# The value tensor of four attention heads: loaded as float32 from another queue and cast on ScalarE, with two buffers instead of three

## The chip, the cores and the metric

The kernel runs on one core of a Trainium2 chip. The core has five engines that run their own instruction streams: TensorE (PE, matrix products), VectorE (DVE), ScalarE (ACT), GpSimd (POOL) and SyncE (SP). Data comes from HBM into the on-chip memory (SBUF) through 16 DMA engines, which all queues share. Transfers can be issued from POOL, whose queue is called software_dynamic in the profile and can change the type of the data on the way, or from SP, whose queue is called hardware_dynamic and copies without a change of type. The metric is the device time of one execution in microseconds (us).

## The reference

The kernel computes an attention block followed by a "soft" mixture of experts. All inputs and the output are float32.

```python
q, k, v: (8 batches, 8 heads, 576 positions, 64)
scores = q @ k.T / 8
# heads 0..3 ("plain"):   position i sees i-31 .. i
# heads 4..7 ("dilated"): position i sees i, i-4, i-8, .. within 128
x = softmax(masked scores) @ v          # -> (4608, 512), heads side by side
logits = x @ phi                        # (4608, 32 slots), 8 experts x 4 slots
slot_input = softmax(logits, over the 4608 rows).T @ x
slot_out[e] = relu(slot_input[e] @ w1[e]) @ w2[e]   # w1 512x1024, w2 1024x512
out = softmax(logits, over the 32 slots) @ slot_out # (4608, 512)
```

## The kernel before

**Units.** The attention is cut into 32 units, four for each batch: two heads each, in the order plain, dilated, plain, dilated (`unit`, L201). The main loop (L475) is a software pipeline. In the turn of unit u it computes the scores of u+1, the weighted values of u (`values`, L324), the exponentials and masks of u+1 (`softmax_parts`, L276), and the transposes of q and k of u+2 (`transposes`, L207); the mixture's logits, row sums and slot sums (`front_logits`, `front_rows`, `front_slots`) follow one batch later. After the loop come the experts (`expert_in`, `expert_out`) and the 40 output tiles (L582 to L600), which SP stores.

**Loads.** Nearly all data is loaded by POOL, float32 in HBM and float16 in SBUF. `load_batch(b)` (L146) issues q and k of the plain heads, then v of the plain heads in five transfers (L168), then q and k of the dilated heads (L163 again), then v of the dilated heads: `vd` (L177) for positions that fill the first 128 rows of four, and `v2r` (L177) for the rest. `load_w(e)` (L192) issues w1 and w2 of one expert, 1 MB each as float16 (L196 and L197). The tiles are eight buffers called home; three of them carry batches in turn and are reused for weights later, so a load into a home waits until the transposes of the batch that was there are done. v of the plain heads goes to one of three `vp` tiles, each with a column of ones that is set once (L121). `v2r` has one buffer: its next load waits until VectorE has copied the last one out.

**Order.** The table `after` (L453) says after which unit each load is issued: batches 0, 1, 2 and expert 0 before the loop; batch 3 after unit 2; batch 4 and expert 1 after unit 6; batch 5 after 10; batch 6 and expert 2 after 14; batch 7 and experts 3 and 4 after 18; experts 5, 6, 7 after 22, 26, 30. The framework that builds the program then orders the instructions of each engine by its own estimate of when they can start, so that an instruction which must wait can be passed by a later one of the same engine. Once built, each engine takes its list strictly in order. In the kernel before, POOL's list is the order of the program text. Each POOL transfer has one of eight semaphores in turn, so that the ninth waits for the first to land.

**Spreading v of the dilated heads.** `spread_v(b)` (L184) copies `vd` and `v2r` on VectorE into the layout that the products need (L187). It stands in the turn of unit 4(b-1)+1, one batch ahead of its use. VectorE takes its list in order, so everything behind such a copy waits for the transfer that the copy waits for.

Of the kernel before, what the change touches and what calls it, by code (L numbers as in the profile page):

```python
# [9 lines left out]
FP32 = mybir.dt.float32  # L10
# [5 lines left out]
B = 8  # L16
H = 8
S = 576
D = 64
# [11 lines left out]
NKB = 5  # L31
# [2 lines left out]
RD, ND = 8, 72  # L34
CL = S // DIL
NU = 4 * B
NV = 3


def constants():  # L40
# [10 lines left out]
def kernel(  # L51
# [10 lines left out]
    nc = tc.nc  # L62
# [17 lines left out]
        out=phi4, in_=phi_sb[:, :, None, :].broadcast_to([128, 4, 4, N_SLOTS])  # L80
# [5 lines left out]
    def kept(shape, name, dt=FP16):  # L86
        return keep.tile(shape, dt, name=name, tag=name)
# [14 lines left out]
    kTd = kept([128, S + 80], "kTd")  # L102
    vp = [kept([128, NKB, 4, D + 1], f"vp{i}") for i in range(NV)]
    vd = [kept([128, 16, D + 1], f"vd{i}") for i in range(2)]
# [10 lines left out]
    for i in range(2):  # L115
# [3 lines left out]
        nc.vector.memset(Er[i][64:128, 8, :], 0.0)  # L119
    for i in range(NV):  # L120
        nc.vector.memset(vp[i][:, :, :, D : D + 1], 1.0)  # L121
# [6 lines left out]
    small = ctx.enter_context(tc.tile_pool(name="small", bufs=2))  # L128
    x_pool = ctx.enter_context(tc.tile_pool(name="x", bufs=2))
    xT_pool = ctx.enter_context(tc.tile_pool(name="xT", bufs=1))  # L130
    vraw_pool = ctx.enter_context(tc.tile_pool(name="vraw", bufs=1))

    big = tc.alloc_tile_pool(name="big", bufs=1)
# [12 lines left out]
    def load_batch(b):  # L146
        t = homes[b_home[b]]
        parts = {}
        at = 0
        for nm, ten, hs, rows, parts_n in (  # L150
            ("qp", q, 0, RP, NP), ("kp", k, 0, RP, NP), ("qd", q, 4, RD, ND), ("kd", k, 4, RD, ND),
        ):
            n = 4 * rows * D
            parts[nm] = t[0:parts_n, at : at + n].rearrange("p (h x) -> p h x", h=4)
            at += n
            src = ten[b, hs : hs + 4].rearrange("h (p r) d -> p h (r d)", r=rows)
            if b == 0 and hs == 0:
                for i in range(2):
                    nc.gpsimd.dma_start(
                        out=parts[nm][:, 2 * i : 2 * i + 2], in_=src[:, 2 * i : 2 * i + 2]  # L160
                    )
            else:
                nc.gpsimd.dma_start(out=parts[nm], in_=src)  # L163
            if nm == "kp":
                vt = vp[b % NV]
                for kb in range(NKB):
                    n_k = 128 if kb < 4 else 64
                    nc.gpsimd.dma_start(  # L168
                        out=vt[0:n_k, kb, :, 0:D],
                        in_=v[b, 0:4, 128 * kb : 128 * kb + n_k, :].rearrange("h p d -> p h d"),  # L170
                    )
        for nm, r0, n_p, dst in (("vd", 0, 128, vd), ("v2", 384, 48, v2)):
            if nm == "vd":
                vr = t[:, 7168:8192].rearrange("p (h x) -> p h x", h=4)
            else:
                vr = vraw_pool.tile([128, 4, 4 * D], FP16, name=f"v2r{b}", tag="v2r")
            nc.gpsimd.dma_start(  # L177
                out=vr[0:n_p],
                in_=v[b, 4:8, r0 : r0 + 4 * n_p, :].rearrange("h (p r) d -> p h (r d)", r=4),
            )  # L180
            parts[nm] = (vr, n_p, dst[b % 2])
        raws[b] = parts

    def spread_v(b):  # L184
        for nm in ("vd", "v2"):
            vr, n_p, dst = raws[b][nm]
            nc.vector.tensor_copy(  # L187
                out=dst[0:n_p, :, 0:D],
                in_=vr[0:n_p].rearrange("p h (r d) -> p (h r) d", r=4),
            )  # L190
# [10 lines left out]
    def unit(u):  # L201
        b, i = divmod(u, 4)
        return b, (0, 2, 1, 3)[i]
# [3 lines left out]
    def transposes(u):  # L207
        b, hp = unit(u)
        for nm in ("q", "k"):
            if nm == "q":  # L210
                dst = qT_pool.tile([128, S], FP16, name=f"qT{u}", tag="qT")
                qTs[u] = dst
            else:
                dst = kTp if hp < 2 else kTd
                kTs[u] = dst
            if hp < 2:
                raw = raws[b][nm + "p"]
                rg = ring.tile([128, RP, NP], FP16, name=f"rg{nm}{u}", tag="ring")
                for r in range(RP):
                    for h in range(2):  # L220
                        nc.tensor.transpose(  # L221
                            rg[64 * h : 64 * h + 64, r, :],
                            raw[:, 2 * hp + h, D * r : D * r + D],
                            ident[0:NP, 0:NP],
                        )
                nc.scalar.copy(  # L226
                    out=dst[:, 0:S].rearrange("c (p r) -> c p r", r=RP),
                    in_=rg.rearrange("c r p -> c p r"),
                )
            else:  # L230
                raw = raws[b][nm + "d"]
                rg = ring.tile([128, 2, 4, ND], FP16, name=f"rg{nm}{u}", tag="ring")
                for h in range(2):
                    for a in range(2):
                        for cc in range(2):
                            nc.tensor.transpose(  # L236
                                rg[:, a, 2 * h + cc, :],
                                raw[:, 2 * (hp - 2) + h, 128 * (2 * a + cc) : 128 * (2 * a + cc) + 128],
                                ident[0:ND, 0:ND],
                            )  # L240
                nc.vector.tensor_copy(  # L241
                    out=dst[:, 0:S].rearrange("c (g p a) -> c g p a", g=4, a=2),
                    in_=rg.rearrange("c a g p -> c g p a"),
                )

    def scores(u):
        b, hp = unit(u)
        qT, kT = qTs[u], kTs[u]
        tiles = []
        for part in range(2):  # L250
            st = ps_s.tile([128, 2, 512], FP32, name=f"s{u}_{part}", tag="s")
            if hp < 2:
                todo = [(160 * i, 128 * i, 128 * i, QW) for i in range(3)] if part == 0 else [
                    (0, 384, 384, QW), (QW, 512, 512, 64)]
            else:
                todo = []
                for cc in range(2):
                    c0 = CL * (2 * part + cc)
                    todo.append((CL * cc, c0, c0, 128))
                    todo.append((CL * cc + 128, c0 + 96, c0 + 128, 16))  # L260
            for at, k0, q0, n in todo:
                for g in range(2):
                    nc.tensor.matmul(  # L263
                        st[:, g, at : at + n],
                        kT[64 * g : 64 * g + 64, k0 : k0 + 128],
                        qT[64 * g : 64 * g + 64, q0 : q0 + n],
                        start=True,
                        stop=True,
                    )
            tiles.append(st)  # L270
        return tiles
# [52 lines left out]
    def values(u):  # L324
# [7 lines left out]
        for half in range(2):  # L332
# [4 lines left out]
            for i, blk in enumerate(blocks):  # L337
                for h in range(2):
                    if plain:
                        P, vt = Pp, vp[b % NV]  # L340
                        mms.append((i, h, P[:, h, blk, 0:128], vt[:, blk, hl + h, :]))
# [123 lines left out]
    def issue(u):  # L465
        for kind, i in after.get(u, ()):
            (load_batch if kind == "b" else load_w)(i)

    issue(-1)
    transposes(0)  # L470
    spread_v(0)
    transposes(1)
    st = scores(0)
    softmax_parts(0, st)
    for u in range(NU + 5):  # L475
        if u + 1 < NU:
            st = scores(u + 1)
        if u < NU:
            values(u)
        if u + 1 < NU:  # L480
            softmax_parts(u + 1, st)
        if u + 2 < NU:
            transposes(u + 2)
        b, ph = divmod(u - 4, 4)
        if 0 <= b < B:
            if ph == 1:
                front_logits(b)
            elif ph == 2:
                front_rows(b)
            elif ph == 3:  # L490
                front_slots(b)
        if 0 <= u - 1 < NU:
            x_transposes(u - 1)
        if u % 4 == 1 and u // 4 + 1 < B:
            spread_v(u // 4 + 1)
        issue(u)
        if u < 4:
            nc.vector.memset(hTp[u], 0.0)

# [82 lines left out]
    for b in range(B):  # L582
        for t in range(NKB):
# [6 lines left out]
            if n % 2 == 0:  # L590
                nc.scalar.activation(  # L591
                    out=ot[0:ns], in_=fp[0:ns], func=AF.Copy, scale=rrow[0:ns, col : col + 1]
                )
            else:
                nc.vector.tensor_scalar(  # L595
                    out=ot[0:ns], in0=fp[0:ns], scalar1=rrow[0:ns, col : col + 1],
# [35 lines left out]
```

## Time and profile before

| | |
|---|---|
| time, median of 3 runs | 215.36 us (214.96 to 216.22) |
| the profiled execution: its time, its span | 216.12 us, 214.3 us |
| mean granted TensorE clock | 0.804 |
| PE busy | 145.2 us (68%) |
| DVE busy | 138.2 us (64%) |
| ACT busy | 92.5 us (43%) |
| POOL busy (issuing transfers) | 77.3 us (36%) |
| read from HBM, written to it | 63.07 MB, 9.44 MB |
| software queue (POOL) | 50336 packets, 31.47 MB |
| hardware queue (SP) | 6208 packets, 9.60 MB |

The span runs from the first to the last instruction; the device time has 1.8 us more around it. The bytes of a queue are those written, so a float32 load that ends as float16 counts half of what it reads. A row of the profile names a source line, the engine, the operation, the tile written and the tiles read, then the busy time and the mean duration of one, then the idle time of that engine just before, with what ended it. The share of a DMA queue is the sum of its packets' durations over 16 engines; it can exceed 100% because an engine has more than one packet under way.

### The profile page before, as it was taken

To read this page: it belongs to the slowest core of one execution; us is meant where nothing else is said; L and a number is where in the kernel's file an instruction comes from. 1 tells how busy PE (TensorE), PEld (TensorE's weight loads), DVE (VectorE), ACT (ScalarE), POOL (GpSimd) and SP (SyncE) were. 2 spreads that over 40 slices of the span, in tenths; PEclk is the share of its full clock that TensorE was granted. 3 is DMA by queue.
4 is the path that set the end of the run, shared out by engine and by line. 5 is a ranking of instruction groups with operands and counts; after the bars stand their busy time and mean duration, and the time that the engine had idled before them with its cause. 6 is when DMAs were issued, how large, how long until landed. Compare 5 with 4: busy or idle time off the path is not lost.

```text
span 214.3 us, 5426 instructions
## 1 busy us (share of the span) xinstructions
PE 145.2 (68%) x2192; PEld 100.0 (47%) x2192; DVE 138.2 (64%) x429; ACT 92.5 (43%) x169; POOL 77.3 (36%) x110
## 2 busy tenths in 40 slices
PE   5448778287609669768767708687886698678740
PEld 4336667165507556556655606566763433211100
DVE  2745987579337997978798419889775301645551
ACT  2234357064604574571744801574542022445550
POOL 7679847512668612747711660300300000000000
PEclk9999999889655997995898755997579669955555
DMA  6999999999999999999999999999999990599995
GB/s 88 163 172 127 179 177 162 205 206 153 151 174 145 200 208 190 146 174 150 202 207 195 136 195 207 213 207 212 206 212 208 213 175 6 197 323 351 356 322 216
DMA packets 56569, 41.41 MB, mean 193 GB/s; under 512 B 23264, under 2 KB 47840, under 8 KB 56544
## 3 DMA queue, kind: packets, MB, share of 16 engines
q0 software_dynamic: 50336, 31.47, 109.3%
q1 hardware_dynamic: 6208, 9.60, 13.0%
q8 instruction: 17, 0.28, 0.5%
q14 instruction: 8, 0.07, 0.1%
HBM read 63.07 MB, written 9.44 MB: 338 GB/s over the span
## 4 chain that ended last, share of the span: by engine, by line
DMA 44%; PE 15%; DVE 13%; issue 12%; POOL 8%; ACT 3%; SPq 2%; DVEq 0%; ACTq 0%; POOLq 0%
DMA home<-in_k_dram 21%; DMA vp<-in_v_dram 7%; DMA out_dram<-ot 6%; DMA home<-in_v_dram 5%; DMA home<-in_q_dram 4%; PE l L392 3%; PE h L531 3%; POOL home L163 3%; DVE ot L595 2%; SPq L599 2%; DVE x L355 2%; PE rgx L374 2%; DVE qT L241 2%; PE sop L555 2%; PE s L263 1%
## 5 line engine op out<-in xcount | busy, mean ns | idle before, releaser
L282 ACT ACTIVATE pr<-s 128x960 f16<-128x960 f32 (+1 forms) x64 | 41.6, 703 | 38.7 <-issue 30.9
L168 POOL DMA_DIRECT2D vp<-in_v_dram x40 | 29.2, 738 | 23.9 <-DMA home<-in_moe_w_dram 11.5
L355 DVE TENSOR_TENSOR x<-o,rc 128x384 f16<-128x384 f32 x64 | 29.6, 485 | 0.3
L350 PE MATMUL o<-vp,Pp 128*128 128x65 f16 x288 | 16.6, 219 | 18.8 <-DVE Pp L288 17.8
L350 PEld LDWEIGHTS <-Pp 128*128 128x128 f16 x288 | 13.5, 113 | 22.6 <-DVE Pp L288 20.7
L374 PE MATMUL rgx<-ident,x 128*128 128x128 f16 x160 | 17.2, 250 | 8.8 <-ACT qT L226 6.5
L595 DVE TENSOR_SCALAR ot<-f,rrow 128x512 f32<-128x512 f32 (+1 forms) x20 | 14.7, 748 | 12.4 <-DMA out_dram<-ot 10.1
L588 PE MATMUL f<-so,ET 128*128 128x512 f16 (+1 forms) x40 | 18.2, 512 | 6.2 <-DVE ot L595 2.8
L399 ACT ACTIVATE ET<-l 128x288 f16<-128x288 f32 x16 | 6.6, 410 | 33.7 <-PE l L392 33.6
L591 ACT ACTIVATE ot<-f,rrow 128x512 f32<-128x512 f32 (+1 forms) x20 | 13.5, 685 | 15.5 <-DMA out_dram<-ot 11.3
L374 PEld LDWEIGHTS <-x 128*128 128x128 f16 x160 | 13.3, 113 | 11.7 <-issue 9.7
L236 PEld LDWEIGHTS <-home 72*128 72x128 f16 x256 | 12.5, 111 | 12.6 <-issue 9.0
L187 DVE COPY vd<-home 128x1024 f16<-128x1024 f16 x8 | 3.4, 425 | 19.6 <-DMA home<-in_v_dram 19.6
L163 POOL DMA_DIRECT2D home<-in_q_dram x15 | 10.8, 721 | 14.3 <-DMA home<-in_moe_w_dram 13.7
L392 PE MATMUL l<-xT,phi 128*128 128x288 f16 x64 | 14.4, 378 | 1.9 <-DVE qT L241 1.6
L350 PEld LDWEIGHTS <-P 128*128 128x128 f16 x256 | 12.3, 106 | 7.1 <-DVE P L305 5.1
L305 DVE TENSOR_TENSOR P<-pr,mask 128x512 f16<-128x512 f16 x32 | 13.4, 420 | 3.0 <-ACT pr L282 3.0
L221 PEld LDWEIGHTS <-home 96*64 96x64 f16 x384 | 13.1, 140 | 4.3 <-issue 1.8
L236 PE MATMUL rgk<-ident,home 72*128 72x72 f16 x128 | 8.5, 221 | 9.3 <-DVE xT L384 8.4
L350 PE MATMUL o<-vd,P 128*128 128x65 f16 x128 | 11.4, 209 | 3.6 <-DVE P L305 3.6
L588 PEld LDWEIGHTS <-ET 128*128 128x128 f16 (+1 forms) x40 | 4.1, 107 | 20.1 <-issue 19.5
L196 POOL DMA_DIRECT2D home<-in_moe_w_dram x8 | 6.1, 757 | 20.1 <-DVE P L305 12.2
(79 smaller groups left out, 286.4 us busy)
## 6 DMA issues: line engine op xcount, KB each, us to landing
home<-in_moe_w_dram POOLq DMA_DIRECT2D x16, 1024.0 KB, 17.8
out_dram<-ot SPq DMA_DIRECT2D x32, 256.0 KB, 3.3
home<-in_q_dram POOLq DMA_DIRECT2D x15, 288.0 KB, 7.8
home<-in_k_dram POOLq DMA_DIRECT2D x15, 288.0 KB, 8.1
home<-in_v_dram POOLq DMA_DIRECT2D x8, 256.0 KB, 7.9
vp<-in_v_dram POOLq DMA_DIRECT2D x32, 64.0 KB, 9.1
out_dram<-ot SPq DMA_DIRECT2D x8, 128.0 KB, 3.3
v2r<-in_v_dram POOLq DMA_DIRECT2D x8, 96.0 KB, 7.5
```

Of the source, the lines that this page charges most:

```text
L163: nc.gpsimd.dma_start(out=parts[nm], in_=src)
L168: nc.gpsimd.dma_start(out=vt[0:n_k, kb, :, 0:D], in_=v[b, 0:4, 128 * kb : 128 * kb + n_k, :].rearrange("h p d -> p h d"),)
L236: nc.tensor.transpose(rg[:, a, 2 * h + cc, :], raw[:, 2 * (hp - 2) + h, 128 * (2 * a + cc) : 128 * (2 * a + cc) + 128], ident[0:ND, 0:ND],)
L282: nc.scalar.activation(out=pr[:, :, 0:n], in_=st[:, :, 0:n], func=AF.Exp, scale=SCALE)
L305: nc.vector.tensor_tensor(out=P1[:, part].rearrange("p c e t -> p e c t"), in0=src[:, :, :, 0:128], in1=bc(mask[:, None, None, 0:128], [12 ...
L350: nc.tensor.matmul(ot[:, i, h, :], lhs, rhs, start=(n == 0), stop=(n == len(mms) - 1))
L355: nc.vector.tensor_tensor(out=x[:, blocks[0] : blocks[0] + nb, D * hl : D * hl + 2 * D].rearrange("p t (h d) -> p t h d", h=2), in0=ot[:, ...
L374: nc.tensor.transpose(rg[:, 128 * blk : 128 * blk + 128], x[:, blk, hl : hl + 128], ident)
L392: nc.tensor.matmul(lp, phi4[:, kc].rearrange("p a s -> p (a s)"), xT[:, kc, 288 * c : 288 * c + 288], start=(kc == 0), stop=(kc == 3),)
L588: nc.tensor.matmul(fp[0:ns], ET[:, r0 : r0 + ns], so, start=True, stop=True)
L591: nc.scalar.activation(out=ot[0:ns], in_=fp[0:ns], func=AF.Copy, scale=rrow[0:ns, col : col + 1])
L595: nc.vector.tensor_scalar(out=ot[0:ns], in0=fp[0:ns], scalar1=rrow[0:ns, col : col + 1], scalar2=None, op0=ALU.mult,)
```

## The change

v of the plain heads no longer goes through POOL's queue. `load_vp(b)` issues the five transfers on SP, as float32, into a staging tile `v32`, of which there is one. `cast_vp(b)` copies it on ScalarE into the `vp` tile, in two instructions (128 rows of 1024 values, 64 rows of 256 values). There are two `vp` tiles instead of three, and two memsets fewer on VectorE (L121 and L122 of the third tile). v of batches 0 and 1 is loaded before the loop, that of batch b+2 after the cast of batch b+1, in the turn of unit 4b+2. The list `after` is unchanged.

```diff
-NV = 3
+NV = 2
@@ pools
+    v32_pool = ctx.enter_context(tc.tile_pool(name="v32", bufs=1))
@@ load_batch
-            if nm == "kp":
-                vt = vp[b % NV]
-                for kb in range(NKB):
-                    n_k = 128 if kb < 4 else 64
-                    nc.gpsimd.dma_start(
-                        out=vt[0:n_k, kb, :, 0:D],
-                        in_=v[b, 0:4, 128 * kb : 128 * kb + n_k, :].rearrange("h p d -> p h d"),
-                    )
@@ after load_batch
+    v32s = {}
+
+    def load_vp(b):
+        t = v32_pool.tile([128, NKB, 4, D], FP32, name=f"v32_{b}", tag="v32")
+        v32s[b] = t
+        for kb in range(NKB):
+            n_k = 128 if kb < 4 else 64
+            nc.sync.dma_start(
+                out=t[0:n_k, kb],
+                in_=v[b, 0:4, 128 * kb : 128 * kb + n_k, :].rearrange("h p d -> p h d"),
+            )
+
+    def cast_vp(b):
+        t = v32s.pop(b)
+        vt = vp[b % NV]
+        nc.scalar.copy(out=vt[:, 0:4, :, 0:D], in_=t[:, 0:4])
+        nc.scalar.copy(out=vt[0:64, 4, :, 0:D], in_=t[0:64, 4])
@@ before the loop
     issue(-1)
+    load_vp(0)
     transposes(0)
+    cast_vp(0)
+    load_vp(1)
     spread_v(0)
@@ in the loop
         issue(u)
+        if u % 4 == 2 and u // 4 + 1 < B:
+            cast_vp(u // 4 + 1)
+            if u // 4 + 2 < B:
+                load_vp(u // 4 + 2)
```

## The prediction

> **What bounds the kernel now.** I read the slices of the page first, then the DMA queues, VectorE's waits, and the timelines of VectorE and POOL towards the end of the attention.
>
> ```profile
> DMA  6999999999999999999999999999999990599995
> GB/s 88 163 172 127 179 177 162 205 206 153 151 174 145 200 208 190 146 174 150 202 207 195 136 195 207 213 207 212 206 212 208 213 175 6 197 323 351 356 322 216
> ...
> q0 software_dynamic: 50336, 31.47, 109.3%
> ...
> DMA 44%; PE 15%; DVE 13%; issue 12%; POOL 8%; ACT 3%; SPq 2%; DVEq 0%; ACTq 0%; POOLq 0%
> ```
>
> From 5 to 177 us the DMA engines never rest. They run at about 210 GB/s written where only weights move and at 130 to 180 where batches move. No compute engine is near full; transfers make up 44% of the chain that ended last. So until 177 us the order in which data comes off the software queue sets the pace. VectorE's waits show where the arithmetic feels it:
>
> ```profile
> DVE vd L187 <- DMA home<-in_v_dram: 19.6, 6, 6.1
> ```
>
> VectorE, in order, stands 19.6 us at the copy of `vd`, 6.1 us the longest time. Its timeline has the last one, batch 7, and the copy of `v2r`, the last piece of that batch:
>
> ```profile
> 121.64 0.18 DVE L354 RECIPROCAL rc<-o 128x6 f32<-128x6 f32 x1
> 127.97 0.43 DVE L187 COPY vd<-home 128x1024 f16<-128x1024 f16 x1 [6.15 <-DMA home<-in_v_dram]
> ...
> 134.86 0.47 DVE L187 COPY v<-v2r 48x1024 f16<-48x1024 f16 x1
> ```
>
> Up to 127.97 the arithmetic waits for batch 7; the second copy at 134.86 finds its data there. From then on only arithmetic is on the path: attention to 166, experts to 183, output tiles to 214.3. From 134.86 to the end is 79.4 us. POOL's timeline tells what had been sent by then:
>
> ```profile
> 119.56 0.77 POOL L177 DMA_DIRECT2D home<-in_v_dram  x1 [0.63 <-DMA home<-in_k_dram]
> 120.62 0.60 POOL L177 DMA_DIRECT2D v2r<-in_v_dram  x1 [0.29 <-DVE P L313]
> 121.40 0.75 POOL L196 DMA_DIRECT2D home<-in_moe_w_dram  x1 [0.18 <-issue]
> 122.52 0.89 POOL L197 DMA_DIRECT2D home<-in_moe_w_dram  x1 [0.38 <-DMA vp<-in_v_dram]
> ```
>
> All eight batches and three experts (0, 1, 2); the weights of expert 3 come behind batch 7.
>
> **The change, part by part.**
>
> *POOL issues 40 transfers less.* The row of L168 has 29.2 us for them. They are taken off no path: POOL waits for landings, not the other way round (13.7 and 11.5 us of its idle time end with a weight's landing). Worth nothing by itself, and covered by the engines' 9s; if these had gaps, it would be worth up to 0.74 us a transfer.
>
> *POOL's list is reordered; this decides.* In the built program the list is no longer the order of the text. With three `vp` waits a batch gone, the builder moves weights ahead of pieces of batches that must wait. The list towards its end, in transfers:
>
> ```
> home(b5) q k q k, vd(b5), vd(b6), w1 w2 of expert 2, v2r(b5),
> q k q k (b6), vd(b7), w1 w2 of expert 3, w1 of expert 4, v2r(b6),
> q k q k (b7), w2 of expert 4, w1 of expert 5, v2r(b7),
> w2 of expert 5, experts 6 and 7
> ```
>
> The software queue delivers in the order of issue: before, the weights issued between two batches held the next batch up, as the 6.10 us and 6.15 us stops at `vd` show. So `v2r` of batch 7 now lands behind all of batches 0 to 7 and five and a half experts, where it was three. VectorE's list still has its copy at the same place, ahead of the masks of unit 26 (before: 134.86). Price: a weight pair is 2.10 MB written (two of 1024 KB). The windows of the trace, with the last two columns the DMA share and GB/s written, give the rate:
>
> ```profile
> 140.00:170.00 30.00, 22.61 (x363) 17.21 (x364) 21.56 (x72) 13.26 (x29) 1.64 (x2) 0.79 1.18 209
> 29.20:31.20 2.00, 1.55 (x27) 1.38 (x24) 1.51 (x6) 0.97 (x2) 0.72 (x1) 1.00 2.07 156
> ```
>
> 2.10 MB / 209 GB/s = 10.0 us an expert. A batch follows by difference: 127.97 - 2 (start) - 3 x 10.0 = 96.0 us for eight, 12.0 us a batch with its plain v.
>
> *Plain v goes to the hardware queue, as float32.* Per batch 2304 rows of 256 B, read as before, but written as 256 B instead of 128 B. Old price: in the window 29.2 to 31.2, nearly all v, 1731 packets under 512 B pass in 2 us, so 2304 take at most 2.7 us; with the few larger ones in it, 2.5 us. The new price is in no row. Low end: 0.59 MB read at the weights' rate (209 GB/s written is 418 read) is 1.4 us. High end: the old packets' own duration, 207% x 16 x 2 us / 1854 = 36 ns, without their twofold overlap: 2304 x 36 ns / 16 = 5.2 us. Nearest are the constants, the hardware queue's only loads:
>
> ```profile
> q1 hardware_dynamic: 822, 0.12, 0.6%
> ```
>
> 0.6% of 16 x 126 us over 822 packets of the stretch 2 to 128 us is 15 ns; 2304 x 15 ns / 16 = 2.2 us. I take 2.2, so 0.3 us less a batch.
>
> *The rest of a batch.* It costs 12.0 - 2.5 = 9.5 us now. By bytes, 2.95 MB read at 418 GB/s, it would be 7.1. Part of the difference comes from POOL's eight places being filled with five small transfers; with six a batch instead of eleven some comes back. Between 9.5 (nothing) and 7.1 (all) I take 9.3, near the present row, as q and k of 72 partitions stay as they are. A batch is then 9.3 + 2.2 = 11.5 us.
>
> *The sum.* `v2r` of batch 7 lands at 2 + 8 x 11.5 + 5.5 x 10.0 = 149 us; the copy was at 134.86: 14.1 us late. Before it, `v2r` of batch 6, behind seven batches, `vd` of batch 7 (1.6 us) and four and a half experts, lands at 2 + 80.5 + 1.6 + 45 = 129 us. One batch of arithmetic takes 16.0 us where nothing waits (the masks of unit 12 to those of unit 16, 73.26 to 89.29), so this stop alone would set 145 to 146.5 with the casts, less than 149. From the copy to the end it is 79.4 us, less 1 us, as the other engines have run ahead to the stop, as ScalarE's next exponentials do.
>
> *ScalarE casts.* 1024 values a batch: the exponential of 960 values takes 973 ns, so 1.04 us; 256 values, by the 410 ns of 288, 0.38 us. 1.4 us a batch on an engine busy 43%. Only the last, in unit 26, lies behind the stop: 0 to 1.4 us, and I take 0.5. Were ScalarE the pace, it would be 11 us over eight.
>
> *One staging tile, two `vp` tiles.* SP waits for cast b+1 before it loads v of b+2; behind it SP has nothing until the outputs. The cast needs it four units (16 us) later, against 1.6 to 3.2 us landings of SP's loads: nothing. A `vp` tile is overwritten four units after its last product: nothing. At the start v of batch 0 shares the engines with q and k; its 2.2 us are in the sum.
>
> *After the attention.* The weights finish no later than before: 2 + 92 + 80 = 174 us against 177, and the experts begin later. The tail keeps its length.
>
> 214.3 + 14.1 - 1 + 0.5 = 228 us of span, 229.7 with the 1.8 around it. The profiled execution (216.12) is 0.76 above the median of the runs, so **229 us**.
>
> *A rule against the hope in this change.* The overlapped packets (207% in the window) say that v in small rows already uses the engines fully, so another queue should free little. The Trainium skill, in "DMA: Bandwidth & Descriptors", section "Issuing engines are not separate DMA queues", goes further: the engine that starts a transfer changes nothing but issue time. By it the batch would stay at 12.0, the landing move to 153, and the time to 233.
>
> **The rivals.**
>
> *Faster: the batch gets cheap.* If a batch fell below (134.86 - 2 - 55) / 8 = 9.7 us, `v2r` of batch 7 would be there in time and the 19.6 us of stops shrink. At the byte price of 8.5 us it lands at 125 and arithmetic decides; with some 3 us of stops saved, 213 us. For it: slices of 130 to 150 GB/s show that batches do not run at the engines' best. Against: it needs 2.3 us of 12.0 a batch, with v moving more bytes.
>
> *The landing comes late but hurts little.* A batch of 9.7 to 10.5 us gives landings of 135 to 141 and 215.5 to 221 us. The 16 us of arithmetic after batch 6's stop, at 115 to 121, then bound it as well.
>
> *The hardware queue is slow with small rows.* At the high end of 5.2 us a batch, 3.0 us over mine, the landing moves by 24 us to 173: some 253 us. For it: 512 rows of 128 B (phi) took 3.2 us to land, 128 rows of 256 B (ident) 1.6. Against: 15 ns a packet.
>
> *The change doesn't do what the list says.* If VectorE could pass the copy, or the weights did not hold `v2r` up, nothing of size would be left: 216 us. Against: VectorE's stops of 6 us.
>
> **How the numbers follow.** Forecast (batch of 10.5 to 12.5 us, 221 to 237) 0.74; cheap batch 0.08; late but harmless 0.08; slow hardware queue 0.07; no effect 0.03. The range from 217 to 238 leaves out the cheap batch, the slow queue, no effect and a part of the harmless case, about 0.2. Faster by over 0.5%, about what a measurement here can tell from no change: 0.08. Within it: the no-effect case and an edge of the harmless one, 0.04. Slower: 0.88.
>
> **What would show it.** Right: VectorE's copies of `v2r` of batches 5, 6 and 7 at about 100, 129 and 149 us, each after a wait of several us that ends with the landing of `v2r`; weights of experts 3 and 4 on the way before batch 7's q; packets on the hardware queue of 10 to 20 ns; 77 to 79 us from the last copy to the end. Wrong, if the last copy comes before 135 us, if DMA slices show gaps before 150 us, or if ScalarE waits for v on SP's queue.

## The result and the profile after

| | before | changed |
|---|---|---|
| median time | 215.16 us (4 runs, 214.21 to 216.22) | 248.8 us (4 runs, 246.01 to 252.56) |
| profiled execution: time, span | 216.12 us, 214.3 us | 246.01 us, 244.2 us |
| end of the attention | 166.1 us | 196.4 us |
| first output transfer | 183.9 us | 214.3 us |

The changed kernel is slower by a factor of 1.145, 95% interval 1.135 to 1.154: 31 us, where 14 were forecast. (Ratios here leave out executions in which the core ran disturbed, so a ratio can differ from the quotient of two medians, which here are 33.6 us apart.) In the profiled executions all of it lies in the attention, which ends 30.3 us later: from its end to the first output it is 17.8 us before and 17.9 us after. By the first exponential of each batch on ScalarE's timeline, batch 1 begins 11.5 us later than before, batch 2 20.5 us, batch 6 37.5 us, batch 7 32.1 us. So two thirds had been lost by the start of the third batch, long before the pieces of batch 7 on which the forecast was built.

The slices, the queues and the chain on the page of the changed kernel:

```profile
DMA  6999979999999999999999999935949900079996
GB/s 101 192 191 172 192 114 170 185 195 192 193 193 200 198 182 189 202 200 196 202 198 209 195 189 207 205 54 98 182 73 183 159 3 0 3 265 343 354 358 231
...
q0 software_dynamic: 31264, 29.11, 74.9%
q1 hardware_dynamic: 25280, 14.32, 25.5%
...
PE 11%; DVE 9%; DMA 7%; issue 4%; ACT 3%; SPq 1%; DVEq 0%; ACTq 0%
```

Apart from the slice from 31 to 37 us, the DMA engines are as full as before up to 159 us. The rate in the slices has not fallen, but v, written as float32, now counts twice in it. From 2 to 159 us the software and the hardware queue wrote 27.92 and 0.12 MB before, 24.65 and 4.85 MB now. With v counted as float16 that is 28.0 against 27.1 MB, some 5 us of transfers. What v costs the engines is thus not what is missing. After 159 us there are gaps: POOL waits there for buffers that the late arithmetic has not given back. The chain is of little use in this kernel: its shares add up to 35%, so most of the span is not on it. The list of waits is what tells. ScalarE's, then SP's (time in all, times, longest):

```profile
ACT vp L193 <- DMA v<-in_v_dram: 39.3, 6, 12.5
ACT vp L192 <- DMA v<-in_v_dram: 15.4, 2, 10.9
```

```profile
SPq L184 <- DMA v<-in_v_dram: 77.1, 18, 12.8
```

ScalarE stands 54.7 us at its casts and waits for the new load, and SP stands at the next loads until the last ones have landed and are cast. ScalarE's row had no counterpart before, and it is the sign that the prediction had named as its refutation. Of VectorE's 19.6 us at `vd` all but the first stop, 3.2 us, are gone. Instead it stands 33.6 us at a copy of TensorE's transposes, and TensorE 29.2 us for ScalarE:

```profile
DVE xT L389 <- PE rgx L385: 33.6, 5, 11.2
```

```profile
PE rgx L385 <- ACT ET L410: 29.2, 5, 9.8
```

ScalarE's `ET` stands directly behind a cast in its list. ScalarE's timeline shows three of the casts, the first with the exponentials around it:

```profile
99.84 1.41 ACT L293 ACTIVATE pr<-s 128x960 f16<-128x960 f32 x2
107.57 0.41 ACT L193 CAST vp<-v 64x256 f16<-64x256 f32 x1 [6.33 <-DMA v<-in_v_dram]
107.88 1.04 ACT L192 CAST vp<-v 128x1024 f16<-128x1024 f32 x1
108.83 0.40 ACT L410 ACTIVATE ET<-l 128x288 f16<-128x288 f32 x1
...
110.51 1.19 ACT L293 ACTIVATE pr<-s 128x576 f16<-128x576 f32 x2 [0.81 <-ACT ET L410]
...
131.26 0.41 ACT L193 CAST vp<-v 64x256 f16<-64x256 f32 x1 [8.21 <-DMA v<-in_v_dram]
131.57 1.04 ACT L192 CAST vp<-v 128x1024 f16<-128x1024 f32 x1
152.63 0.41 ACT L193 CAST vp<-v 64x256 f16<-64x256 f32 x1 [5.41 <-DMA v<-in_v_dram]
```

The casts are 23.7 and 21.4 us apart. SP's timeline has the loads between them:

```profile
108.95 3.44 SPq L184 DMA_DIRECT2D v<-in_v_dram  x4
...
132.64 6.88 SPq L184 DMA_DIRECT2D v<-in_v_dram  x5
```

The load of the next batch leaves as soon as the cast has emptied the one staging tile (131.57 + 1.04 = 132.6), and the next cast begins 20 to 22 us later, when the load has landed. So the loop of load and cast sets the pace of the attention: some 22 us a batch, where a batch of arithmetic without a stop takes 16.

One thing more makes a late v costly. The cast at 107.57 is that of batch 5. In the program text it comes behind the exponentials of unit 19; in ScalarE's built list it stands between those of unit 14 (99.84) and unit 15 (110.51), so five units of arithmetic that do not need this v wait for it. At the start too: the cast of batch 3, at 62.72, had waited 12.5 us, and the first exponential of batch 2, at 69.38, came behind it. No run moves the casts back, so how much of the loss their place makes is not known.

Why does a load take 20 us that alone takes three? The DMA queues in three stretches of the changed kernel (packets, MB, share of 16 engines). From 38 to 39.5 us, v with an empty software queue:

```profile
q1 hardware_dynamic: 1142, 0.28, 84.4%
q0 software_dynamic: 2, 0.00, 1.0%
```

From 92 to 94 us, v beside smaller rows of POOL's queue:

```profile
q0 software_dynamic: 442, 0.25, 87.0%
q1 hardware_dynamic: 440, 0.11, 45.1%
```

From 98 to 102 us, v beside weights, with rows of 2 KB:

```profile
q0 software_dynamic: 397, 0.71, 95.2%
q1 hardware_dynamic: 394, 0.10, 19.1%
```

Alone, 1142 packets pass in 1.5 us: 2304 take 3.0 us, and this load, issued at 35.7, had landed whole at 42.3. With both queues full, the packets that pass are the same number on both sides, 442 to 440 and 397 to 394, whatever their size. That is what a taking of turns, packet by packet, would give. A batch's v has 2304 packets of 256 B, and by this reading each waits for one of the other queue's, up to 2 KB and seven times as many bytes per turn in the last stretch; at 394 in 4 us the whole load would take 23 us, at 440 in 2 us 10. In the load issued at 86.27 the first packets pass at 90 and the last at 107: 4 us until it starts, 17 us of turns. The Trainium skill states the rule in "DMA: Bandwidth & Descriptors", section "Queues, rings and completion order": an engine goes round its queues and drains one packet of a ring before it switches. A packet there is a group of several descriptors, while the profile counts one packet for each row, so the counts agree with equal shares but do not show how many rows make a turn.

### The profile page after: what moved, and what is told of

Its sections match the earlier page's. It is cut to its first block, busy times and chain, and to the rows that moved or that the text cites. A ratio compares the mean times of both kernels' runs of the same rounds, so it can differ in the third digit from the quotient of the medians.

```text
span 244.2 us, 5469 instructions
## 1 busy us (share of the span) xinstructions
PE 154.6 (63%) x2192; PEld 107.8 (44%) x2192; DVE 138.7 (57%) x427; ACT 102.1 (42%) x185; POOL 47.8 (20%) x70
## 5 line engine op out<-in xcount | busy, mean ns | idle before, releaser
L385 PE MATMUL rgx<-ident,x 128*128 128x128 f16 x160 | 19.4, 273 | 36.4 <-ACT ET L410 29.2
L361 PE MATMUL o<-vp,Pp 128*128 128x65 f16 x288 | 17.0, 225 | 17.8 <-DVE Pp L299 17.2
L389 DVE COPY xT<-rgx 128x576 f16<-128x576 f16 x16 | 7.3, 457 | 33.9 <-PE rgx L385 33.6
L193 ACT CAST vp<-v 64x256 f16<-64x256 f32 x8 | 3.3, 407 | 39.3 <-DMA v<-in_v_dram 39.3
L361 PEld LDWEIGHTS <-P 128*128 128x128 f16 x256 | 13.9, 116 | 6.7 <-DVE P L316 3.9
L247 PEld LDWEIGHTS <-home 72*128 72x128 f16 x256 | 14.4, 124 | 5.1 <-DMA home<-in_q_dram 2.8
L299 DVE TENSOR_TENSOR Pp<-pr,mask 128x960 f16<-128x960 f16 x16 | 10.3, 644 | 10.5 <-ACT pr L293 10.5
L170 POOL DMA_DIRECT2D v2r<-in_v_dram x8 | 4.8, 597 | 56.8 <-DVE v L198 37.4
L192 ACT CAST vp<-v 128x1024 f16<-128x1024 f32 x8 | 8.4, 1046 | 15.4 <-DMA v<-in_v_dram 15.4
L403 PE MATMUL l<-xT,phi 128*128 128x288 f16 x64 | 12.0, 322 | 2.2 <-DVE qT L252 1.9
L252 DVE COPY qT<-rgq 128x576 f16<-128x576 f16 x16 | 12.0, 752 | 2.5 <-PE rgq L247 2.5
```

Source lines behind the costliest of these rows:

```text
L247: nc.tensor.transpose(rg[:, a, 2 * h + cc, :], raw[:, 2 * (hp - 2) + h, 128 * (2 * a + cc) : 128 * (2 * a + cc) + 128], ident[0:ND, 0:ND],)
L252: nc.vector.tensor_copy(out=dst[:, 0:S].rearrange("c (g p a) -> c g p a", g=4, a=2), in_=rg.rearrange("c a g p -> c g p a"),)
L361: nc.tensor.matmul(ot[:, i, h, :], lhs, rhs, start=(n == 0), stop=(n == len(mms) - 1))
L385: nc.tensor.transpose(rg[:, 128 * blk : 128 * blk + 128], x[:, blk, hl : hl + 128], ident)
L403: nc.tensor.matmul(lp, phi4[:, kc].rearrange("p a s -> p (a s)"), xT[:, kc, 288 * c : 288 * c + 288], start=(kc == 0), stop=(kc == 3),)
```

## The experiments

Two theories stood after the result. T (turns): the load is long because its packets take turns, and the loop through the one staging tile sets the pace. L (list): the forecast's own mechanism, pieces of the batches that land behind weights issued ahead of them. The expectations also weigh B: float32 bytes, or the hardware queue's small rows, cost the engines their time.

**Fewer, larger packets.** Same bytes, same queue, same staging tile, but v is read in rows of 1 KB: 768 packets a batch instead of 2304. The rows of v come out permuted, so the product is another one.

```diff
-            nc.sync.dma_start(
-                out=t[0:n_k, kb],
-                in_=v[b, 0:4, 128 * kb : 128 * kb + n_k, :].rearrange("h p d -> p h d"),
-            )
+            if kb < 4:
+                nc.sync.dma_start(
+                    out=t[:, kb].rearrange("p h d -> p (h d)"),
+                    in_=v[b, kb, 0:512, :].rearrange("(p r) d -> p (r d)", r=4),
+                )
...
```

> The changed kernel with v of the plain heads fetched in rows of 1 KB: 768 packets a batch on SP's queue instead of 2304, the same bytes, staging tile, casts and instruction lists. (It leaves out the right order of v's rows in the tile, so the product is made with permuted rows; the work is the same.) Theory T (turns): the DMA engines take one packet from SP's queue for one from POOL's, so v's load lasts as long as 2304 POOL packets take, about 21 us, and with one staging tile the loop load, cast, load sets 22 us a batch. It expects the load to land in 7 to 9 us, ScalarE's waits for v to fall from 55 us to under 10, and what is left to be set by other things: 215 to 232 us. Theory L (list, the forecast's): v2r of batch 7 behind five and a half experts sets the end; the size of v's packets hardly matters: within 4 us of the changed kernel's 249, or, if both hold, 225 to 232 with a wait of VectorE at the last copy of v2r. Theory B (the hardware queue's bytes, float32 instead of float16): no change, 245 to 252.

Measured: 226.88 us, ratio 1.036 (1.028 to 1.044), where the changed kernel has 1.145: three quarters of the loss are gone. The queues from 94 to 97 us show the turns again:

```profile
q0 software_dynamic: 379, 0.39, 75.8%
q1 hardware_dynamic: 377, 0.34, 42.6%
```

A turn of v now carries three and a half times the bytes. The first half of B falls, as neither bytes nor queue changed; what small rows cost the engines is left to the next run. ScalarE's stops for v shrink from 54.7 to 14.0 us, the longest 4.2 (T said under 10 in all), and VectorE stops where the forecast had put it, at the copy of `v2r` of batch 6. From the list of its waits:

```profile
DVE v L203 <- DMA v2r<-in_v_dram: 8.2, 2, 7.6
```

That copy was at 127.1 us (forecast: 129). The copy for batch 7, at 143.7 us, found its data there. Below the loop lay the list.

**A second staging tile.** v of batch b+3 is loaded after the cast of b+1. Room for the tile comes from the expert tiles `hTp`, which move into the memory of the mask tile `Pp` and are cleared after the attention.

```diff
-    v32_pool = ctx.enter_context(tc.tile_pool(name="v32", bufs=1))
+    v32_pool = ctx.enter_context(tc.tile_pool(name="v32", bufs=2))
@@ before the loop
     load_vp(0)
+    load_vp(1)
...
     cast_vp(0)
-    load_vp(1)
+    load_vp(2)
@@ in the loop
-            if u // 4 + 2 < B:
-                load_vp(u // 4 + 2)
+            if u // 4 + 3 < B:
+                load_vp(u // 4 + 3)
```

> The changed kernel with two staging tiles, v loaded one batch further ahead; to make room in the SBUF, the four small expert tiles lie in the mask tile of the plain heads, which is done by then, and their four memsets come after unit 31. Theory T: a load of 21 us has 32 us to land, the loop is cut, casts of batches 3 to 7 find their data: ScalarE's waits for v under 15 us, 215 to 235 us in total. Theory L alone: the list behind POOL is almost the same, so 245 to 252; T and L together: about 229, with VectorE waiting for v2r of batch 7 until about 149 us. Theory B (engines lose time to the small float32 packets): the weights finish later, 245 us or more.

Measured: 235.09 us, ratio 1.081 (1.075 to 1.087). The turns are the same, only a load has a batch more time. All the small rows are still there, so the rest of B falls as well: it said 245 us or more. ScalarE stands 18.4 us at three casts at the start (T said under 15) and no longer waits for v after 38 us. VectorE's timeline, copies of `v2r` of batches 5, 6 and 7:

```profile
110.30 0.42 DVE L201 COPY v<-v2r 48x1024 f16<-48x1024 f16 x1 [5.54 <-DMA v2r<-in_v_dram]
...
133.90 0.42 DVE L201 COPY v<-v2r 48x1024 f16<-48x1024 f16 x1 [5.99 <-DMA v2r<-in_v_dram]
...
154.04 0.42 DVE L201 COPY v<-v2r 48x1024 f16<-48x1024 f16 x1 [3.98 <-DMA v2r<-in_v_dram]
```

This is the picture that the prediction described, stop for stop, each 5 to 10 us later than forecast (100, 129 and 149), with 80 us from the last to the end. It is what the change costs if the loop of load and cast is slack. Only part of it is the list: at batch 1 this kernel is already 13.3 us late, before any stop at `v2r`, and by ratio the list is worth 5%, as the run with both mended shows below.

**Two `vp` tiles alone.** The kernel before with `NV = 2` and all loads on POOL.

```diff
-NV = 3
+NV = 2
```

> The kernel before with two v tiles instead of three and nothing else: POOL still loads v as float16. In POOL's built list v2r of batch 7 then stands behind expert 3 and the first half of expert 4, some 15 us of transfers further back than before. Theory L: its copy on VectorE moves from 134.9 us to about 143, 221 to 226 us in total. Theory T: no loop without SP's queue, and if lists do not matter, 214 to 217 us.

Measured: 228.82 us, ratio 1.054 (1.049 to 1.059). Batch 2's v is loaded before the loop over that of batch 0, so batch 0 is computed with the wrong v; the work is the same. The size is near what L expected (221 to 226 us), but the stop is elsewhere. TensorE's longest item in the list of waits:

```profile
PE o L350 <- DMA vp<-in_v_dram: 22.4, 10, 9.9
```

Batch 1 begins at 38.7 us instead of 28.8, so this kernel is late from the start. It proves nothing for L.

**Half rows.** The changed kernel with each row of 256 B as two of 128 B: 4608 packets a batch.

```diff
-            nc.sync.dma_start(
-                out=t[0:n_k, kb],
-                in_=v[b, 0:4, 128 * kb : 128 * kb + n_k, :].rearrange("h p d -> p h d"),
-            )
+            for d0 in (0, 32):
+                nc.sync.dma_start(
+                    out=t[0:n_k, kb, :, d0 : d0 + 32],
+                    in_=v[b, 0:4, 128 * kb : 128 * kb + n_k, d0 : d0 + 32].rearrange("h p d -> p h d"),
+                )
```

> The changed kernel with each 256 B row of v fetched as two rows of 128 B: 4608 packets a batch on SP's queue, the same bytes. Theory T: the load lasts as long as POOL's queue has packets to alternate with, 28 to 40 us instead of 21; the loop becomes 28 us a batch or more: 275 to 310 us. A fixed cost of each packet of 15 to 21 ns on 16 engines would give 2.2 to 3.0 us a batch: 266 to 273 us. Theory L and theory B: within 5 us of the changed kernel's 249.

Measured, in a single execution: 270.15 us, ScalarE's stops for v 38.7 + 36.8 = 75.5 us. Slower with the same bytes, but less than T's range said. From 88 to 92 us the queues show why: the turns hold only while the software queue has work, and POOL issued nothing between 74.3 and 89.3 us.

```profile
q0 software_dynamic: 540, 0.44, 71.9%
q1 hardware_dynamic: 2276, 0.28, 53.4%
```

Here four packets of v pass for each of POOL's. A fixed cost per packet would have given the same time, so this run doesn't separate the two.

**The list alone.** The kernel before, with two experts issued ahead of batch 7.

```diff
-        18: (("b", 7), ("w", 3), ("w", 4)),
+        18: (("w", 3), ("w", 4), ("b", 7)),
```

> The kernel before, with the weights of experts 3 and 4 issued ahead of batch 7 instead of behind it; three v tiles, POOL loads v. Nothing else is changed. Theory L (a piece of a batch lands behind all weights issued before it, and VectorE's copy then holds the arithmetic): 20 us of transfers more ahead of batch 7, so vd of batch 7 lands at 147 to 149 us instead of 128; its copy now stands just ahead of the masks of unit 26, which were at 136.8, so 11 to 12 us later: 226 to 230 us. If the order in the list costs nothing: 214 to 219 us.

Measured: 227.41 us, ratio 1.053 (1.045 to 1.062). VectorE's timeline at batch 7:

```profile
146.64 0.43 DVE L187 COPY vd<-home 128x1024 f16<-128x1024 f16 x1 [16.59 <-DMA home<-in_v_dram]
```

The copy moves from 127.97 to 146.64 us, 18.7 us for two experts (forecast price: 20). The mechanism of the list is real, and its price per expert right.

**Two `v2r` buffers in the changed kernel.** With a second buffer POOL needn't wait for VectorE's copy, so the pieces of a batch go out ahead of the weights. The loop stays.

```diff
-    vraw_pool = ctx.enter_context(tc.tile_pool(name="vraw", bufs=1))
+    vraw_pool = ctx.enter_context(tc.tile_pool(name="vraw", bufs=2))
```

> The changed kernel with two buffers for v2r, so that its loads no longer wait for VectorE and the builder puts v2r of batch 7 behind four experts instead of five and a half. SP's loads, the one staging tile and the casts are as in the changed kernel. Theory T (turns and loop): the loop of 22 us a batch still sets the pace: 243 to 252 us, ScalarE's waits for v still 45 us or more. Theory L alone: 15 us of transfers less ahead of the last piece: 232 to 238 us.

Measured: 253.21 us, ratio 1.176 (1.164 to 1.188). ScalarE's waits:

```profile
ACT vp L193 <- DMA v<-in_v_dram: 31.6, 5, 10.2
ACT vp L192 <- DMA v<-in_v_dram: 27.3, 3, 12.1
```

58.9 us of stops at the casts, 4 more than in the changed kernel; the time lies just above T's range. While the loop stands, mending the list gains nothing. That it got slower fits T (POOL's queue is fuller, so v takes turns for longer), but that was not measured apart.

**Both mended, twice.** The second `v2r` buffer, once with two staging tiles and once with the rows of 1 KB (permuted as above): each is the edit shown above plus the `vraw` line.

> Two staging tiles (as in the run with two stages, with the expert tiles in the mask tile) and two buffers for v2r. Theories T and L together: the loop is cut and v2r of batch 7 stands behind four experts: 2 + 8 x 12.3 + 40 = 140 us, copy at 140, 79 us from there: 217 to 225 us. If the list is not what holds the run with two stages at 235 us, it stays at 231 to 237.

> Rows of 1 KB for v (as before, the rows of v are permuted, so the product is not the reference's; the work is the same), one staging tile, and two buffers for v2r. Theories T and L together: neither the loop nor the list holds much: v2r of batch 7 lands at 2 + 8 x 11.5 + 40 = 134 us, where the kernel before copies it at 134.9: 214 to 220 us. If something else holds the run with big rows at 225 us: 222 to 228.

Measured: 222.12 us, ratio 1.029 (1.019 to 1.040), and 214.58 us, ratio 0.981 (0.968 to 0.995). The table holds all six ratios to the kernel before:

| v's load | one `v2r` buffer | two |
|---|---|---|
| one staging tile, 256 B rows | 1.145 | 1.176 |
| two staging tiles | 1.081 | 1.029 |
| one staging tile, 1 KB rows | 1.036 | 0.981 |

The second buffer is worth 5% in the rows where the loop is slack and nothing in the first. The two causes do not add up, which fits that each batch waits for the later of the two.

**Two `v2r` buffers in the kernel before**, as the control.

```diff
-    vraw_pool = ctx.enter_context(tc.tile_pool(name="vraw", bufs=1))
+    vraw_pool = ctx.enter_context(tc.tile_pool(name="vraw", bufs=2))
```

> The kernel before with two v2r buffers; nothing else. Control for the runs in which the second v2r buffer stood in the changed kernel. If L is right about the kernel before (it waits for vd, 19.6 us in six stops, and not for v2r), the second buffer moves nothing of size: 213 to 217 us, within 1% of before. If v2r's single buffer were also what holds POOL's list in the kernel before, the stops at vd would shrink and the time fall to 208 to 212.

Measured: ratio 1.001 (0.996 to 1.006). POOL's list has no weights ahead of a batch's `v2r` here, as it has in the changed kernel, and the buffer is worth nothing.

**Weights later.** If the list sets the pace, it should also be possible to gain by it. The kernel before with two experts moved back:

```diff
-        6: (("b", 4), ("w", 1)),
-        10: (("b", 5),),
-        14: (("b", 6), ("w", 2)),
-        18: (("b", 7), ("w", 3), ("w", 4)),
+        6: (("b", 4),),
+        10: (("b", 5), ("w", 1)),
+        14: (("b", 6),),
+        18: (("b", 7), ("w", 2), ("w", 3), ("w", 4)),
```

> The kernel before with expert 1 issued behind batch 5 instead of batch 4, and expert 2 behind batch 7 instead of batch 6; the reverse of the run that put weights first. L: vd of batch 7 lands one expert (10 us) earlier, that of batches 5 and 6 too; VectorE's stops at vd (19.6 us in all, 6.1 at batch 7) mostly go, and 5 to 8 us of them are won at the end, if the weights, which finish at 177 as before, do not become the wait: 207 to 212 us. If arithmetic between the stops is what decides, no more than 2 us: 213 to 216. If POOL now stands at homes that are not yet free, engines would idle and the weights would come later: 216 to 222.

Measured: 214.08 us, ratio 0.992 (0.989 to 0.995): 0.8%. L's 207 to 212 us is missed; it is the case in which the arithmetic between the stops decides. The stop at `vd` of batch 7 is gone, and that copy is at 123.95 instead of 127.97 us. Then the same with two `v2r` buffers:

> The last two edits together: expert 1 behind batch 5 and expert 2 behind batch 7, two v2r buffers, v still through POOL's queue with three vp tiles. L: with the batches' pieces earlier, the single v2r buffer would be POOL's next stop; with two it is none: 206 to 211 us. If the second buffer is worth nothing, the time is that of the run with one, within 1 us.

Measured: 213.57 us, ratio 0.982 (0.978 to 0.987), the lowest ratio of the kernels that neither leave out nor permute anything. The DMA row of its slices:

```profile
DMA  5999999999999999999999999999999992699995
```

The weights come without a gap to 175 us. L's range is missed again. With one buffer the built list had one expert's weights ahead of `v2r` of batch 7, with two it has none; but the copies of that `v2r` start at 130.68 and 130.50 us, so why the second buffer helps here stays open.

**The same later weights in the changed kernel** with two staging tiles and two `v2r` buffers:

> The changed kernel with two staging tiles, two v2r buffers (222.1 us) and the same later places of experts 1 and 2. T and L leave some 6 us over the kernel before in that kernel. If these are still order of landing, v2r and vd of batches 5 to 7 come earlier and the time falls to 212 to 218. If they are the cost of v on SP's queue and of the casts (turns between the queues while batches and weights land, ScalarE's copies between the exponentials), nothing moves: 220 to 224.

Measured: 222.11 us, ratio 1.030 (1.025 to 1.035), as without the move. What is left over the kernel before is not the place of these weights. ScalarE's timeline shows where some of it arises, at the start:

```profile
25.92 1.05 ACT L195 CAST vp<-v 128x1024 f16<-128x1024 f32 x1 [4.93 <-DMA v<-in_v_dram]
...
38.33 0.41 ACT L196 CAST vp<-v 64x256 f16<-64x256 f32 x1 [8.74 <-DMA v<-in_v_dram]
...
42.69 1.41 ACT L296 ACTIVATE pr<-s 128x960 f16<-128x960 f32 x2
```

Batch 1's first exponential is at 42.69 us, where it was at 28.8, as the cast of batch 2 stands ahead of it in ScalarE's list and waits 8.74 us. At batch 2 the delay is 11.5 us, and it shrinks to 5 us by batch 7. How the rest divides between turns, the casts' own 1.4 us a batch and their place in ScalarE's list stays open.

## Why the prediction was wrong

The direction was right and the time was not: 229 us with a range from 217 to 238 stand against 248.8.

- *One staging tile, two `vp` tiles: "The cast needs it four units (16 us) later, against 1.6 to 3.2 us landings of SP's loads: nothing."* This is the step that failed. The landings were read from rows at the start of the kernel, where POOL's queue had hardly begun, and were used for loads that run beside a full one. Beside it a batch's v takes 20 to 22 us, against 16 us of arithmetic, and ScalarE stood 54.7 us at the casts. The built list was read for POOL and not for ScalarE, where the casts had moved ahead of arithmetic that does not need them. With a second staging tile and the list left as it is, the same change takes 235.09 us, inside the range given; but part of that is a late start, which the prediction did not have.
- *"A `vp` tile is overwritten four units after its last product: nothing."* In the built list the cast comes right behind that product. In the three runs with a slack loop and two `v2r` buffers ScalarE stands about 7 us in four such stops, up to 1.8 us each; one of the three is at 0.981, so this did not decide.
- *Plain v goes to the hardware queue.* 2.2 us were taken, and alone it measured 3.0. The sum used that figure as a share of the engines' time, which is right for throughput, and the DMA slices stayed full as forecast. That a load's latency is another quantity, set here by how much passed beside it, had no term.
- *POOL's list is reordered; this decides*, and *The sum.* The mechanism is real: the run with weights first gives 18.7 us for two experts, and stops at `v2r` appear once the loop is slack: for batch 6 at 127.1 us with larger rows, for batches 6 and 7 at 133.9 and 154.0 us with two staging tiles, where 129 and 149 were forecast. In the changed kernel itself it was covered: the copies were at 120.9, 145.0 and 166.4 us without any wait. So it did not decide.
- *From the copy to the end*: 77.8 us (244.2 - 166.36) for 78.4. Right.
- *ScalarE casts*: 1.05 and 0.41 us for 1.04 and 0.38. Right, and of no weight beside the waiting.
- *POOL issues 40 transfers less*: nothing gained, as said. POOL's idle time moved to waits for copies and for homes.
- *After the attention*: the weights end at about 195 us instead of the 174 forecast, by the slices, as homes came free late. The tail kept its length all the same.
- The rival "the hardware queue is slow with small rows" gave 253 us, near the result, for a reason that the runs contradict: it charged the engines 5.2 us a batch, which alone measured 3.0, and would have moved the landing in POOL's queue. The engines' time was not the matter: with the same packets on the same queue, a second staging tile brought the ratio from 1.145 to 1.081.
- The Trainium skill's "DMA: Bandwidth & Descriptors", section "Issuing engines are not separate DMA queues", says that transfers of all engines interleave, which the counts show, and that the issuing engine changes only issue time. Here the issuing engine also decided in which queue v takes its turns, and so when it lands: 20 to 22 us after issue instead of with its batch. The 233 us worked out by that rule missed as well.

The views that would have told of it were at hand in part. The prediction asked what v costs the engines, but not how long a load stays under way beside a queue that never runs empty, though 5 to 177 us of 9s in the DMA slices say that it would always run beside one.

## What to carry to other kernels

Before moving a load to another queue, count its packets and those that pass beside it: two full queues went packet for packet here, so a load of many small rows beside one of large rows lands late though it costs the engines little. A single staging buffer makes that latency the period of the loop (load, cast, load); compare it with the time of one turn, and give the load a second buffer or larger rows. Look in the built list where the instruction stands that will wait for the load, and what stands behind it. And when one cause hides another, mend each with the other mended as well: alone, the second `v2r` buffer looked worthless here, and with the loop slack it was worth 5%.

## What the runs showed of the hardware

- Two queues that both have work passed the same number of packets, 442 to 440, 397 to 394, 379 to 377. The software queue's were of 0.6, 1.8 and 1.0 KB on average, the hardware queue's of 0.25, 0.25 and 0.9 KB. Where the software queue ran short (71.9% of the engines), it was 540 to 2276.
- 256 B rows from HBM on the hardware queue alone: 16 x 1.5 us / 1142 = 21 ns a packet and engine, with the engines 84.4% busy.
- The first packets of a load issued beside a full software queue passed 4 us after the issue (86.27 to 90). Which part of the way that is, no run shows.
